# Class-1 tiles of the second mixer product: weights read from w2 itself instead of from a packed copy

## The chip, the core and the metric

The kernel runs on one core of a Trainium2 chip. The metric is the device time of one execution in microseconds. Lower is better. The engines are named as in the profile: PE is TensorE (PEld its weight loads), DVE is VectorE, ACT is ScalarE, POOL is GpSimd and SP is SyncE. SP computes nothing; it issues most of the DMAs. Each engine runs its own list of instructions in an order that is fixed when the program is built. An instruction that waits holds back everything behind it on its engine.

## What is computed

Two layers, each an attention block A and a token mixer B on x of 2048 tokens by 1024 channels (bf16), with the same weights in both layers:

```
x = x + A(layernorm(x), wqkv, wo)     # 32 heads of 32; 8 keys per query, 2 tokens apart
x = x + B(layernorm(x), w1, b1, w2, b2)

def B(x, w1, b1, w2, b2):
    h = layernorm(x)
    u = gelu(einsum("bsd,sf->bdf", h, w1) + b1)     # mixes the 2048 tokens into 3584
    y = einsum("bdf,fs->bds", u, w2) + b2           # and back: w2 is 3584 x 2048
    return y transposed to (token, channel)
```

## The kernel before, in words

**Classes.** A query sees keys two tokens apart, so even tokens (class 0) and odd tokens (class 1) never meet in the attention. The kernel works on the two classes apart, each 1024 tokens in NT = 8 tiles of 128. Column s of w2 belongs to token s, so the class-0 columns of w2 are its even columns and the class-1 columns its odd ones.

**The mixer.** gemm1 (L672) makes g, the 3584 x 1024 activations, in 14 blocks of 256 rows. gemm2_tile(c, i, ...) (L697) makes one output tile: 128 tokens of class c by 1024 channels. It is 28 steps over the 3584 rows with two matmuls each (one per 512 channels), so 56 matmuls. The weights of a step are 128 columns of w2, the moving operand is g. The 28 steps are cut into NW2 = 4 quarters of HF = 7 steps, 14 matmuls each. At the end DVE adds bias and residual out of PSUM (L711), POOL stores the tile (L717), the tile is normalised for the next attention (on ACT with stats_act and norm_act for class-1 tiles 0 to 5, on DVE for the others) and SP issues the transposing DMA to hT (to_hT, L236).

**Where the tiles run.** In layer 0 the eight class-0 tiles of gemm2 run one after the other behind gemm1 (L883). The eight class-1 tiles of layer 0 are held back: they are the fill "second" (second_class, L847) inside the attention of layer 1. There weave (L755), a planner with a modelled time for PE and for DVE, puts the pieces of such fills between the attention's own units, so that PE has work while DVE does the attention's elementwise part. Layer 1's gemm2 (L886) takes both classes of a tile from one load of w2.

**How w2 gets on the chip.** There are two ways:

- w2_tiles(i) (L730) loads 256 neighbouring columns of w2, both classes of tile i, in four DMAs of 448 KB. Each row of such a DMA is 512 bytes. A quarter is one DMA and one buffer. The weights are then read with a step of 2 columns, c::DIL (L741).
- w2_kept(i) (L743) loads the class-1 columns alone from a packed copy in DRAM, w2_odd[i], in two DMAs of 448 KB with rows of 3584 bytes. A DMA covers two quarters. The weights are read without a step.

The packed copy is made on the way: with keep=True, w2_tiles lets ACT copy the odd columns of each quarter into a tile `odd` (L737) and store that to w2_odd[i] from ACT's queue (L740). `odd` takes a buffer of the pool tpl, whose two buffers also serve the attention's T and pr.

**Buffers.** All these loads take buffers from the pool wbp, five of 4 KB per partition, in turn. So do wv (L378), wo (L620) and w1 (L668). A load is issued when the buffer that it is given has been read for the last time. The residual rows xr, the normalised tile hb and others share the pool x2p, four buffers (L79); q, k and v projections of the attention take their weights wq from a pool of their own (wqp, three buffers), and SP issues those loads too (L390).

**Queues.** SP's list holds the loads of w2, w1, wq, wv, wo and xr and the transposing DMAs; POOL's holds the attention's probabilities (pd written at L473, pb read back at L487, 1 MB each) and the stores of output tiles; ACT's holds the stores of `odd`.

Of the kernel before, what the change touches and what calls it, by code (L numbers as in the profile page):

```python
# [15 lines left out]
P = 128  # L16
# [10 lines left out]
def kernel(  # L27
# [21 lines left out]
    NT = SC // P  # L49
# [57 lines left out]
    def bank(name="ps"):  # L107
        return psp.tile([P, 512], FP32, name=name, tag="ps")

    def x2(name, shape=None, dt=BF16):  # L110
        return x2p.tile(shape or [P, D], dt, name=name, tag="x2")
# [61 lines left out]
    xb = [dram.tile([SC, D], BF16, name=f"xb{c}") for c in range(DIL)]  # L173
# [35 lines left out]
    def stats_act(x, mul, eps, junk, sums=None):  # L209

        s1 = sums
        if s1 is None:
            s1 = st("s1", [P, NDC])
            for n in range(NDC):
                nc.scalar.activation(out=junk[:, n * 512:(n + 1) * 512], in_=x[:, n * 512:(n + 1) * 512],  # L215
                                     func=ACT.Identity, accum_out=s1[:, n:n + 1])
        t1 = st("t1", [P, 1])
        nm = st("nm", [P, 1])
        nc.scalar.activation(out=t1[:], in_=s1[:, 1:2], func=ACT.Copy, scale=-1.0 / D)
        nc.scalar.activation(out=nm[:], in_=s1[:, 0:1], func=ACT.Identity, bias=t1[:], scale=-1.0 / D)  # L220
        ss = st("ss", [P, 1])
        nc.scalar.activation(out=junk, in_=x, func=ACT.Square, bias=nm[:], accum_out=ss[:])  # L222
        rs = st("rs", [P, 1])
        rsqrt(rs[:], ss[:], mul / D, eps)
        return nm, rs

    def norm_dve(dst, x, mean, rs, op=ALU.subtract):
        nc.vector.tensor_scalar(out=dst, in0=x, scalar1=mean, scalar2=rs[:], op0=op, op1=ALU.mult)

    def norm_act(dst, x, nm, rs):  # L230
        bi = st("bi", [P, 1])
        nc.scalar.activation(out=bi[:], in_=nm[:], func=ACT.Identity, scale=rs[:])
        nc.scalar.activation(out=dst, in_=x, func=ACT.Identity, bias=bi[:], scale=rs[:])  # L233
# [463 lines left out]
    def gemm2_tile(c, i, w2t, xs, dst, hT, on_act=False, end=False):  # L697
        xo = xs.take()
        halves = [slice(n * 512, (n + 1) * 512) for n in range(NDC)]
        groups = [halves[:1], [slice(512, 768)], [slice(768, 1024)]] if end else [halves]  # L700
        for cols in groups:
            acc = [bank() for _ in cols]
            for n in range(NW2):
                for ft in range(n * HF, (n + 1) * HF):
                    for ps, xc in zip(acc, cols):
                        nc.tensor.matmul(ps[:, 0:xc.stop - xc.start], lhsT=w2t(ft, c),  # L706
                                         rhs=g[ft // GF][:, ft % GF, xc], start=(ft == 0), stop=(ft == FT - 1))
                if n < NW2 - 1:
                    yield 1.5 * len(cols), 0.0
            for ps, xc in zip(acc, cols):  # L710
                nc.vector.scalar_tensor_tensor(out=xo[:, xc], in0=ps[:, 0:xc.stop - xc.start], scalar=b2_sb[:, i, c:c + 1],  # L711
                                               in1=xo[:, xc], op0=ALU.add, op1=ALU.add)
            yield 1.5 * len(cols), 0.75 * len(cols)
            if end:
                nc.sync.dma_start(out=dst[:, cols[0]], in_=xo[:, cols[0]])
        if not end:
            nc.gpsimd.dma_start(out=dst, in_=xo[:])  # L717
        if hT is None:
            return
        hb = x2("hb")  # L720
        if on_act:
            nm, rs = stats_act(xo[:], 1.0, eps1, hb[:])
            norm_act(hb[:], xo[:], nm, rs)
        else:
            mean, rs = stats_dve(xo[:], 1.0, eps1)
            norm_dve(hb[:], xo[:], mean, rs)
        to_hT(hb[:], hT, c, i)
        yield 0.0, 0.0 if on_act else 2.0

    def w2_tiles(i, keep=False):  # L730
        tiles = []
        odd = tpl.tile([P, NW2, HF, P], BF16, name="odd", tag="T") if keep else None
        for n in range(NW2):
            t = wb("w2", [P, HF, FB])
            nc.sync.dma_start(out=t[:], in_=w2_v[:, n * HF:(n + 1) * HF, i * FB:(i + 1) * FB])
            if keep:
                nc.scalar.copy(out=odd[:, n], in_=t[:, :, 1::DIL])  # L737
            tiles.append(t)
        if keep:
            nc.scalar.dma_start(out=w2_odd[i].rearrange("p (f m) -> p f m", m=P), in_=odd[:].rearrange("p n f m -> p (n f) m"))  # L740
        return lambda ft, c: tiles[ft // HF][:, ft % HF, c::DIL]  # L741

    def w2_kept(i):  # L743
        tiles = []
        for n in range(2):
            t = wb("w2", [P, FT // 2, P])
            nc.sync.dma_start(out=t[:].rearrange("p f m -> p (f m)"), in_=w2_odd[i][:, n * F // 2:(n + 1) * F // 2])
            tiles.append(t)
        return lambda ft, c: tiles[ft // (FT // 2)][:, ft % (FT // 2), :]

    def run(*its):
        for _ in chain(*its):
            pass
# [68 lines left out]
    hT = [[None, None] for _ in range(DIL)]  # L822
    new_hT(hT, 0)
    for li in range(2):
        first = li == 0
        at_ = Attn(li, hT, 0 if first else 2)
        h2 = [[None, None] for _ in range(DIL)]
        res = [xin_v[c] for c in range(DIL)] if first else [rows(xb[c]) for c in range(DIL)]

        def clear_pads():  # L830
            for t in v_g:
                nc.gpsimd.memset(t[:, :, 0:PADK + 2], 0.0)

        def opening():
            for i in range(NT):
                x_stage(0, i)
            load_biases()
            clear_pads()
            with tc.manual_schedule(engines={getattr(mybir.EngineType, e) for e in ("PE", "DVE", "Activation", "Pool")}):
                first_tiles(hT, partial(at_.project, 0))  # L840
                for i in range(NT):
                    x_stage(1, i)
            yield "at", 27.0, 29.0
            for u in ((1, 2, 1), (1, 3, 1), (0, 2, 0),):
                yield from at_.proj(0, *u)

        def second_class():  # L847
            new_hT(hT, 1)
            xs = Rows([rows(xa[0][1])[i] for i in range(NT)], 1)
            for i in range(NT):  # L850
                if first:
                    prologue_tile(1, i, hT)
                    yield 0.0, 2.0 * (i % 2 == 0)
                else:
                    yield from gemm2_tile(1, i, w2_kept(i), xs, xb[1][i * P:(i + 1) * P, :], hT, on_act=i < NT - 2)

        def v_ahead():
            if not first:
                clear_pads()
            for pair in range(KD // 2):  # L860
                for unit in at_.proj_pair(1, pair, (2,)):
                    yield 1.75, 0.0

        def partials(lo, hi):
            for fb in range(lo, hi):
                yield from gemm1(h2, fb, (0,), True, False)

        lead = chain(at_.stream(opening() if first else None), out_proj(at_, 1, res[1], xa[li][1], h2, on_act=False))
        weave(lead, {"second": second_class(), "v_ahead": v_ahead(),
                     "out0": out_proj(at_, 0, res[0], xa[li][0], h2, on_act=True),  # L870
                     "partials": partials(0, NFB - KD), "late": partials(NFB - KD, NPART)},
              {"second": 25.0} if first else {})
        for fb in range(NPART, NFB):
            run(gemm1(h2, fb, (0, 1), True, True))
        for fb in range(NPART):
            run(gemm1(h2, fb, (1,), False, True))
        if first:
            with at(top):
                ln_exp_table()
            hT = [[None, None] for _ in range(DIL)]  # L880
            new_hT(hT, 0)
            xs = Rows([rows(xa[0][0])[i] for i in range(NT)], 1)
            for i in range(NT):  # L883
                run(gemm2_tile(0, i, w2_tiles(i, keep=True), xs, xb[0][i * P:(i + 1) * P, :], hT))
        else:
            xs = Rows([rows(xa[1][c])[i] for i in range(NT) for c in range(DIL)], 1)  # L886
            for i in range(NT):
                w2t = w2_tiles(i)
                for c in range(DIL):
                    run(gemm2_tile(c, i, w2t, xs, out_v[c, i], None, end=(i == NT - 1 and c == DIL - 1)))  # L890
# [30 lines left out]
```

## Time and profile before

Four runs gave 1291.75 to 1295.67 us, median 1292.99 us.

| | before |
|---|---|
| profiled execution, its own time | 1292.17 us |
| its span, first to last instruction | 1290.4 us |
| PE busy | 1264.0 us (98%) |
| DVE busy | 680.4 us (53%) |
| ACT busy | 502.7 us (39%) |
| DMA | 173.01 MB, mean 134 GB/s |
| ACT copies to `odd` (L737) | x32, 30.0 us |
| loads by w2_tiles (L735) | x64, 448.0 KB each, median 3.8 us to landing |
| loads by w2_kept (L747) | x16, 448.0 KB each, median 3.8 us to landing |
| stores of `odd` (L740) | x8, 896.0 KB each, median 5.7 us to landing |

How to read it: span is the time from the first to the last instruction, and 1.8 us of the execution lie around it. A row of busy time counts an engine's instructions without the waits between them. The trace gives every time from the start of the span: the class-0 tiles of layer 0 run from 457 us to about 554 us, the class-1 tiles of layer 0 from about 568 us to 748 us.

### The profile page before, as it was taken

The page shows a single profiled execution, that of the slowest core. Times are in us where ns is not written, and L with a number is a line of the kernel's source. Part 1 is how long each engine was busy: PE and PEld are TensorE (multiplying, and loading weights), DVE is VectorE, ACT ScalarE, POOL GpSimd, SP SyncE. Part 2 cuts the span into 40 slices and gives each one's busy share as a digit, 9 for nine tenths or more (in the row PEclk, how much of TensorE's full clock was granted, in tenths as well). Part 3 has the DMA queues.
Part 4 walks back from the last instruction along what each step waited for, and adds up shares of the span by engine and source line. Part 5 has one row for each costly group of instructions (what it writes and reads, how often), then busy time and mean ns, then how long its engine had stood idle before and what let it go on. Part 6 is the DMA issues. An engine that isn't in the chain of part 4 may idle for free. (4 is left out here: it accounts for less than half of the span.)

```text
span 1290.4 us, 15498 instructions
## 1 busy us (share of the span) xinstructions
PE 1264.0 (98%) x6163; PEld 574.9 (45%) x6284; DVE 680.4 (53%) x861; ACT 502.7 (39%) x836; POOL 60.9 (5%) x166
## 2 busy tenths in 40 slices
PE   8999999999999999999999999999999999999999
PEld 4344444444444444444444444444444444444444
DVE  6879899979013422335896734978920233011011
ACT  6845446635324433325414535484343344000000
POOL 3000001001000000000000000010000000000000
PEclk9999999999999999999999999999999999999999
DMA  9852436563422289943647652349262222334331
GB/s 254 187 122 84 120 107 164 165 154 106 139 82 82 60 230 297 288 149 95 156 119 185 158 140 84 73 140 227 67 178 74 74 82 73 122 120 135 104 112 53
DMA packets 217817, 173.01 MB, mean 134 GB/s; under 512 B 32080, under 2 KB 198352, under 8 KB 215696
## 3 DMA queue, kind: packets, MB, share of 16 engines
q1 hardware_dynamic: 206768, 126.11, 36.1%
q0 software_dynamic: 9248, 37.51, 10.5%
q10 hardware_dynamic: 1728, 8.39, 1.7%
q8 instruction: 49, 0.80, 0.3%
q14 instruction: 24, 0.20, 0.0%
HBM read 139.47 MB, written 26.21 MB: 128 GB/s over the span
## 5 line engine op out<-in xcount | busy, mean ns | idle before, releaser
L682 PE MATMUL ps<-h,w 128*128 128x512 bf16 x1756 | 386.7, 379 | 4.8 <-ACT h L233 2.1
L706 PE MATMUL ps<-g,w 128*128 128x512 bf16 (+1 forms) x1785 | 388.0, 376 | 3.0 <-ACT v L419 1.2
L706 PEld LDWEIGHTS <-w 128*128 128x128 bf16 x1820 | 177.5, 98 | 212.4 <-issue 5.6
L682 PEld LDWEIGHTS <-w 128*128 128x128 bf16 x1792 | 175.0, 98 | 215.8 <-issue 4.6
L412 PE MATMUL ps<-hT,wq 128*128 128x512 bf16 (+1 forms) x1085 | 241.4, 374 | 4.3 <-DVE xr L711 0.9
L693 DVE TENSOR_TENSOR tmp<-ps,g 128x512 f32<-128x512 f32 x96 | 66.4, 692 | 211.2 <-PE ps L682 207.0
L711 DVE SCALAR_TENSOR_TENSOR xr<-ps,b_sb,xr 128x512 bf16<-128x512 f32 (+1 forms) x65 | 45.6, 736 | 234.9 <-PE ps L706 196.2
L444 DVE TENSOR_TENSOR T<-q,k 128x4096 bf16<-128x4096 bf16 x60 | 135.5, 2285 | 63.9 <-ACT q L416 52.5
L412 PEld LDWEIGHTS <-wq 128*128 128x128 bf16 x1112 | 108.4, 100 | 132.0 <-issue 13.1
L509 DVE TENSOR_TENSOR pr<-pr 128x2048 bf16<-128x2048 bf16 (+1 forms) x128 | 119.2, 946 | 0.2
L694 ACT ACTIVATE g<-tmp,b_sb 128x512 bf16<-128x512 f32 x96 | 69.2, 721 | 93.2 <-DVE tmp L693 92.8
L412 PE MATMUL ps<-hT,wv 128*128 128x512 bf16 x436 | 100.6, 380 | 1.0 <-issue 0.5
L631 PE MATMUL ps<-wo,oT 128*128 128x512 bf16 x377 | 89.1, 379 | 2.4 <-DMA wo<-in_A_wo_dram 2.0
L688 ACT CAST g<-ps 128x512 bf16<-128x512 f32 x96 | 55.2, 590 | 91.4 <-PE ps L682 85.6
L419 ACT CAST k<-ps 128x1024 bf16<-128x1024 f32 x60 | 60.7, 1014 | 73.5 <-PE ps L412 70.1
L505 DVE TENSOR_TENSOR pr<-pb,v 128x2048 bf16<-128x2048 bf16 x64 | 75.9, 1214 | 20.8 <-DMA pb<-pd 10.8
L505 DVE TENSOR_TENSOR pr<-pb,g 128x2048 bf16<-128x2048 bf16 x64 | 76.3, 1215 | 12.1 <-DMA pb<-pd 12.1
L412 PEld LDWEIGHTS <-wv 128*128 128x128 bf16 x448 | 48.6, 112 | 50.5 <-issue 7.2
L631 PEld LDWEIGHTS <-oT 128*128 128x128 bf16 x384 | 37.2, 98 | 48.4 <-issue 4.3
L416 ACT CAST q<-ps 128x512 bf16<-128x512 f32 x60 | 34.8, 584 | 47.8 <-PE ps L412 47.8
L419 ACT CAST g<-ps 128x1024 bf16<-128x1024 f32 x36 | 36.6, 1016 | 40.9 <-PE ps L412 40.9
L737 ACT COPY odd<-w 128x896 bf16<-128x896 bf16 x32 | 30.0, 937 | 55.1 <-DMA w<-in_B_w_dram 54.9
(91 smaller groups left out, 606.2 us busy)
## 6 DMA issues: line engine op xcount, KB each, us to landing
w<-in_B_w_dram SPq DMA_DIRECT2D x56, 512.0 KB, 4.2
w<-in_B_w_dram SPq DMA_DIRECT2D x64, 448.0 KB, 3.8
wq<-in_A_wqkv_dram SPq DMA_DIRECT2D x38, 512.0 KB, 4.2
pb<-pd POOLq DMA_DIRECT2D x16, 1024.0 KB, 10.3
wo<-in_A_wo_dram SPq DMA_DIRECT2D x16, 512.0 KB, 3.9
xa<-xr POOLq DMA_DIRECT2D x32, 256.0 KB, 3.2
xr<-xa SPq DMA_DIRECT2D x32, 256.0 KB, 3.8
wv<-in_A_wqkv_dram SPq DMA_DIRECT2D x14, 512.0 KB, 5.7
```

The costliest lines, as they stand in the source:

```text
L412: nc.tensor.matmul(ps[:, lo:hi], lhsT=cols, rhs=self.hT[c][hf][:, kt, lo:hi], start=(kt == 0), stop=(kt == KD - 1))
L419: nc.scalar.copy(out=window(buf, 0, PADK + hf * HT, [(KW + 1, 2), (1, HT)]), in_=ps[:].unsqueeze(1).to_broadcast([P, 2, HT]))
L444: nc.vector.tensor_tensor(out=T[:], in0=q.unsqueeze(1).to_broadcast([P, 4, SC]), in1=window(k, par, 2, [(2, 4), (1, SC)]), op=ALU.mult)
L505: nc.vector.tensor_tensor(out=pr[:, :, u, :], in0=pb[:, :, u, :], in1=window(self.v_of(c, dt), par, 2 + hf * HT, [(TB, 4), (2, 4), (1, TB) ...
L509: nc.vector.tensor_tensor(out=pr[:, :, 0:wd, :], in0=pr[:, :, 0:wd, :], in1=pr[:, :, wd:2 * wd, :], op=ALU.add)
L631: nc.tensor.matmul(banks[(i, n)][:], lhsT=at_.oT[c][kt][:, i * P:(i + 1) * P], rhs=wo_t[n][kt // 4][:, kt % 4, :], start=(kt == 0), stop=( ...
L682: nc.tensor.matmul(ps[:], lhsT=wt[c][:, i, fl * P:(fl + 1) * P], rhs=h2[c][i // 4][:, i % 4, dc * 512:(dc + 1) * 512], start=(k == 0), sto ...
L688: nc.scalar.copy(out=gs, in_=ps[:])
L693: nc.vector.tensor_tensor(out=tmp[:], in0=ps[:], in1=gs, op=ALU.add)
L694: nc.scalar.activation(out=gs, in_=tmp[:], func=ACT.Gelu_apprx_tanh, bias=b1_sb[:, ft:ft + 1])
L706: nc.tensor.matmul(ps[:, 0:xc.stop - xc.start], lhsT=w2t(ft, c), rhs=g[ft // GF][:, ft % GF, xc], start=(ft == 0), stop=(ft == FT - 1))
L711: nc.vector.scalar_tensor_tensor(out=xo[:, xc], in0=ps[:, 0:xc.stop - xc.start], scalar=b2_sb[:, i, c:c + 1], in1=xo[:, xc], op0=ALU.add, ...
```

## The change

The class-1 tiles of layer 0 call w2_tiles(i) in place of w2_kept(i), and the class-0 tiles call it without keep. So nothing is packed and nothing is stored to w2_odd, and the class-1 tiles load 256 columns of w2 in four DMAs and read every second column. The functions themselves are as before; w2_kept and the packing branch are called by nothing any more.

```diff
@@ second_class @@
-                    yield from gemm2_tile(1, i, w2_kept(i), xs, xb[1][i * P:(i + 1) * P, :], hT, on_act=i < NT - 2)
+                    yield from gemm2_tile(1, i, w2_tiles(i), xs, xb[1][i * P:(i + 1) * P, :], hT, on_act=i < NT - 2)
@@ layer 0, behind gemm1 @@
-                run(gemm2_tile(0, i, w2_tiles(i, keep=True), xs, xb[0][i * P:(i + 1) * P, :], hT))
+                run(gemm2_tile(0, i, w2_tiles(i), xs, xb[0][i * P:(i + 1) * P, :], hT))
```

## The prediction

> **What bounds the kernel now.** First the page, for the engine that is never idle.
>
> ```profile
> PE 1264.0 (98%) x6163; PEld 574.9 (45%) x6284; DVE 680.4 (53%) x861; ACT 502.7 (39%) x836; POOL 60.9 (5%) x166
> ```
>
> PE is the bound, and busy means at its pace: the timeline has 49 matmuls in 10.74 us, 0.219 us each, wherever it runs freely. So an edit counts only by what PE waits. Next, busy time by stage: class-0 tiles; layer 1's attention with the class-1 tiles, cut in four.
>
> ```profile
> 460.00:550.00 90.00, 89.58 (x410) 40.80 (x417) 23.49 (x42) 29.19 (x43) 3.78 (x7) 1.00 1.00 281
> 555.00:640.00 85.00, 83.29 (x440) 35.82 (x447) 51.10 (x45) 36.86 (x53) 2.77 (x5) 1.00 0.47 125
> 640.00:675.00 35.00, 34.20 (x177) 15.21 (x180) 34.06 (x38) 5.63 (x6) 1.02 (x2) 1.00 0.33 103
> 675.00:700.00 25.00, 24.45 (x112) 11.63 (x114) 14.98 (x19) 13.63 (x28) 1.76 (x4) 1.00 0.98 229
> 700.00:757.00 57.00, 55.27 (x251) 25.39 (x255) 34.63 (x46) 22.86 (x48) 3.63 (x13) 1.00 0.60 161
> ```
>
> Columns: stretch, length, then busy us of PE, PEld, DVE, ACT, POOL; clock; DMA share; GB/s. In the first row the DMA engines are full (1.00) while PE loses 0.42 us in 90. In the other four it loses 1.71 + 0.80 + 0.55 + 1.73 = 4.79 us. Third, PE's waits in 555 to 760 us (us in all, times, longest):
>
> ```profile
> PE ps L706 <- ACT v L419: 1.2, 2, 0.7
> PE ps L412 <- DVE xr L711: 0.9, 1, 0.9
> PE ps L412 <- DMA wq<-in_A_wqkv_dram: 0.9, 1, 0.9
> ```
>
> None is for a w2 load. Fourth, SP's timeline, which the change fills (start, length, line, what, count):
>
> ```profile
> 680.16 0.32 SPq L747 DMA_DIRECT2D w<-w2o  x1
> 682.32 3.35 SPq L236 DMA_TRANSPOSE hT<-hb  x1
> 690.92 0.33 SPq L608 DMA_DIRECT2D xr<-xa  x1
> ...
> 698.96 0.32 SPq L608 DMA_DIRECT2D xr<-xa  x1
> 713.60 1.24 SPq L236 DMA_TRANSPOSE hT<-hb  x1
> 714.94 0.52 SPq L747 DMA_DIRECT2D w<-w2o  x1
> ...
> 725.63 0.34 SPq L608 DMA_DIRECT2D xr<-xa  x1
> 736.42 1.23 SPq L236 DMA_TRANSPOSE hT<-hb  x1
> ```
>
> SP stands still from 699.3 to 713.6 us and from 726.0 to 736.4 us. The cause, from SP's waits in 560 to 757 us:
>
> ```profile
> SPq L236 <- ACT hb L233: 32.4, 5, 14.3
> ```
>
> The transposing DMA of a tile waits for its normalised hb; that waits for L711 on DVE, which is behind with the attention (34.06 of 35 us busy). A w2 load listed behind such a transpose waits too.
>
> **The change, part by part.**
>
> *Removed: packing.* 32 copies of 0.937 us take 30.0 us off ACT, 8 stores of 896 KB leave its queue, and `odd` leaves the pool of T. All this lies beside the class-0 tiles, where PE loses 0.42 us: that is the most it gives. I take 0. There the DMA should fall from 281 GB/s by 7.3 MB in 90 us, 82 GB/s, to some 200.
>
> *Weights at a step of two columns.* PE's count is unchanged, 448 matmuls. The trace has both forms, first class 0 (step 2) in 460 to 550 us, then class 1 (packed) in 655 to 673 us:
>
> ```profile
> L706 PEld LDWEIGHTS <-w 128*128 128x128 bf16 x417 | 40.8, 98 | 49.2
> L706 PEld LDWEIGHTS <-w 128*128 128x128 bf16 x84 | 8.2, 98 | 9.9
> ```
>
> Behind the bar stand busy us and mean ns: 98 ns both, under a pace of 219 ns. Cost 0. Only wv's step of 4 shows a dearer load (page: 112 ns), still below the pace.
>
> *Added: bytes.* 32 loads of 448 KB for 16: 7.3 MB more, all in 555 to 757 us, where 28 MB move now (560 to 757 us). At the full-DMA row's 281 GB/s that is 26 us of DMA in 202 us at about half use. Only 675 to 700 us has no room (0.98). About 1.4 MB more should fall there (12 loads for the 6 from 659 to 697 us; half of the surplus lands in it), 5 us at 281 GB/s. There ACT already waits 5.0 us for a store of xb behind the two pb loads, and holds the v casts that PE waits 1.2 us for. Bounds on PE: 0 (buffers absorb it) to 5 us. I take 0: of the 10.1 us that this store needs now, PE shows about 1 us.
>
> The Trainium skill, "DMA: Bandwidth & Descriptors", Specifications, speaks against any cost of short rows: a transfer of 512 B or more runs at line rate, about 27 GiB/s per engine. By that estimate the extra bytes need 16 us of 16 engines instead of the 26 us above; this case's full-DMA row, 281 GB/s with rows of mostly 512 B, does not reach that rate, so the row decides.
>
> *Added: SP's issues.* 32 at 0.37 us for 16 at 0.34 us is 6.4 us more on a queue that waits most of the time. Cost 0 by itself.
>
> *Moved: the lead of a load.* This is the term I keep. All loads take wbp's five buffers in turn. A load waits until the one five before it is used up, so its lead is four loads' worth of PE work: four halves, 56 x 2 x 0.216 = 24.2 us, before; four quarters, 12.1 us, after. The load lands 3.8 us after issue (at most 6.6 us by w2_tiles, 9.8 us by w2_kept). So SP may be 8.3 us late before PE waits. Before, it could be 20.4 us late.
>
> In the class-0 stage the same five buffers serve the same loads at full pace and PE waits for none, but there hb is normalised by an idle DVE and SP's longest wait on hb is 2.6 us. Here the holds are 14.3 and 10.4 us. I follow the ring by hand from the counts of L706 in PE's timeline, quarters of 14 matmuls, tiles numbered from 0.
>
> - Hold to 713.6 us. Tile 4's first quarter is used up at 694.0 us; its buffer is for tile 5's second quarter, needed at 714.8 us. Ahead of the held transpose it lands by 702 us. Behind it: 713.6 + 1.3 + 3.7 = 718.6 us, 3.8 us late. The next quarters (buffers free at 697.0 and 699.9 us) would land about 719 and 720 us, needed at 717.8 and 720.8 us: hidden by the first delay.
> - Hold to 736.4 us. Tile 6's first quarter is used up at 726.8 us, just after the hold begins; its buffer is for tile 7's second quarter, needed at 738.9 us. Behind the hold: 736.4 + 1.3 + 5 (between the 3.7 us of L747 and the 6.1 us of the wv beside it) = 742.7 us, 3.8 us late.
> - Hold from 685.7 to 694.9 us (xr, then a transpose). The load of tile 4's last quarter can go at 696.2 us, lands at 700.5 us, is needed at 703.5 us: in time.
>
> Each is late only if the new list puts the load behind the transpose. That list is not in the trace. For: before, the loads at 714.94 and 723.54 us stand right behind a transpose although the first one's buffer was free at 706.3 us. Against: a quarter's load comes due more often, so some find a place ahead. Bounds: 0, and both, 7.6 us. I take one, **3.8 us**, as the row before shows both orders.
>
> Sum on the profiled execution: 1292.2 + 0 + 0 + 0 + 3.8 = **1296.0 us**, 3.0 us above the median of 1293.0 us (the execution lies 0.8 us below that).
>
> **The rivals.** A measurement here tells about 0.2%, 2.6 us, from no change.
>
> 1. *No load is late.* The loads stand ahead of the held transposes, as five buffers suffice in the class-0 stage; PE's waits stay as they are. 1292.2 + 0 = 1292 to 1293 us. For it: no PE wait for w2 anywhere in 455 to 760 us. Against: holds above the 8.3 us allowance.
> 2. *Faster: the stage's waits for banks go.* PE's waits around 675 and 711 us come from class-1 tiles whose xr and hb hold up DVE and ACT while PE runs ahead. A later arrival of w2 spaces these tiles; with packing gone the lists are also made anew. Price: at most the 4.8 us that PE loses in the stage, 1292.2 - 4.8 = 1287.4 us; with the two waits on L419 and the one on L711 gone as the gaps in the rows show, 1.2 + 0.9 plus the refill of its pace, about 3 us, 1289 us. It decides if the first tiles, at 640 to 675 us, are spread and not bunched. Against: the order of the fills in weave uses the same modelled costs.
> 3. *The DMA burst at 675 to 700 us decides as well.* Both loads late and the burst's 5 us: 1292.2 + 7.6 + 5 = 1304.8 us. For: 0.98 use there. Against: 0.47 and 0.33 before it, so loads can go early.
>
> **How the numbers follow.** Forecast (one or two loads late) 0.42; rival 1 0.32; rival 2 0.18; rival 3 0.08. Faster by over 0.2% is rival 2: 0.18. Within it is rival 1: 0.32. Slower is the forecast and rival 3: 0.50. The range goes from 1289 us, rival 2's likelier price, to 1305 us, rival 3. The forecast's own range is 1294.8 to 1300 us (2.6 to 7.6 us).
>
> **What would show it.** No L737 and no L740; w2 loads x96 by L735; weight loads of L706 at 98 ns in both stages; DMA in the class-0 stage near 200 GB/s and PE idle there under 0.5 us. In 640 to 757 us a wait of PE for DMA w<-in_B_w_dram of 3 to 8 us in one or two pieces, each behind a late transpose in SP's timeline. I am wrong if PE's waits in 555 to 760 us hold no w2 load, if the time moves outside that stretch, or if L706's loads go above the pace.

## The result, and the profile after

| | before | after |
|---|---|---|
| median of the runs (lowest to highest) | 1294.6 us (1291.75 to 1300.39, 69 runs) | 1297.1 us (1294.83 to 1301.41, 45 runs) |
| ratio, 95% interval | | 1.0020 [1.0014, 1.0025] |
| profiled execution, its own time | 1292.17 us | 1297.12 us |
| its span | 1290.4 us | 1295.0 us |

The change costs 0.20%, 2.5 us. The two profiled executions differ by more, 4.6 us of span: the one of before lies near the low end of its runs. So the profiles say where time goes, and the runs how much: sums by place below are against that one execution of before and come out larger than the change in the runs.

The page of after, in the rows that answer to those of before:

```profile
PE 1264.7 (98%) x6163; PEld 574.8 (44%) x6284; DVE 680.5 (53%) x861; ACT 473.9 (37%) x804; POOL 60.9 (5%) x166
...
L706 PEld LDWEIGHTS <-w 128*128 128x128 bf16 x1820 | 177.3, 98 | 215.2 <-issue 7.2
...
w<-in_B_w_dram SPq DMA_DIRECT2D x96, 448.0 KB, 3.8
```

ACT's busy time fell by 28.8 us (the packing), PE's work is the same, a weight load of the mixer takes 98 ns, and all 96 loads of w2 come from w2 itself. The busy time by stage of after, in the same stretches and columns as before:

```profile
460.00:550.00 90.00, 89.58 (x411) 40.78 (x418) 23.49 (x42) 3.49 (x14) 3.78 (x7) 1.00 0.80 215
555.00:640.00 85.00, 82.94 (x439) 35.61 (x446) 51.12 (x45) 37.01 (x53) 2.77 (x5) 1.00 0.52 136
640.00:675.00 35.00, 34.05 (x176) 15.18 (x179) 33.67 (x37) 5.47 (x6) 0.63 (x1) 1.00 0.50 147
675.00:700.00 25.00, 23.66 (x108) 11.23 (x110) 11.99 (x16) 13.64 (x28) 2.15 (x4) 1.00 1.04 238
700.00:757.00 57.00, 52.96 (x240) 24.02 (x244) 37.47 (x49) 21.69 (x46) 3.64 (x13) 1.00 0.87 225
```

In the class-0 stage the DMA fell from 281 to 215 GB/s and PE gained nothing. In the class-1 stage PE loses 2.06 + 0.95 + 1.34 + 4.04 = 8.39 us where it lost 4.79 us, 3.1 of the 3.6 us of increase behind 675 us. PE's waits of after in 640 to 770 us (us in all, times, longest):

```profile
PE ps L706 <- ACT v L419: 2.5, 3, 0.9
PE ps L412 <- DVE xr L711: 2.2, 2, 1.3
PE ps L706 <- DMA w<-in_B_w_dram: 0.7, 1, 0.7
```

A load of w2 is now late, but by 0.7 us only. The waits for ACT and DVE grew instead, from 1.2 and 0.9 us. Where, says PE's timeline, first of before, then of after:

```profile
685.15 15.27 PE L706 MATMUL ps<-g,w 128*128 128x512 bf16 x69
...
706.73 3.62 PE L412 MATMUL ps<-hT,wq 128*128 128x512 bf16 x16
710.83 0.38 PE L706 MATMUL ps<-g,w 128*128 128x512 bf16 x1 [0.48 <-ACT v L419]
711.92 36.20 PE L706 MATMUL ps<-g,w 128*128 128x512 bf16 x164 [0.72 <-ACT v L419]
```

```profile
684.99 6.42 PE L706 MATMUL ps<-g,w 128*128 128x512 bf16 x29
692.36 9.01 PE L706 MATMUL ps<-g,w 128*128 128x512 bf16 x40 [0.95 <-ACT v L419]
...
709.17 3.61 PE L412 MATMUL ps<-hT,wq 128*128 128x512 bf16 x16 [1.32 <-DVE xr L711]
713.66 0.38 PE L706 MATMUL ps<-g,w 128*128 128x512 bf16 x1 [0.87 <-ACT v L419]
714.75 30.46 PE L706 MATMUL ps<-g,w 128*128 128x512 bf16 x136 [0.72 <-ACT v L419]
745.95 6.22 PE L706 MATMUL ps<-g,w 128*128 128x512 bf16 x28 [0.73 <-DMA w<-in_B_w_dram]
```

PE's list has the same order in both kernels, so its 6284 weight loads can be paired and their starts subtracted. After minus before is -0.5 us until 630 us and -0.15 us from there to 690 us. Then it jumps: +1.11 at 692.4, +1.49 at 709.2, +0.39 at 713.7, +0.3 at 730, +0.9 at 746, +0.39 at 759.7 us, together 4.6 us; behind that only 0.2 us more comes. So, against this execution of before, PE loses in two places: **2.99 us at 692 to 714 us** (the burst), and **1.6 us at 730 to 760 us** (late quarters and what follows them). I call these sums the first and the second step.

**The second step** is in SP's timeline of after:

```profile
731.85 0.39 SPq L735 DMA_DIRECT2D w<-in_B_w_dram  x1
739.25 1.23 SPq L236 DMA_TRANSPOSE hT<-hb  x1
740.58 1.19 SPq L735 DMA_DIRECT2D w<-in_B_w_dram  x2
```

The load at 731.85 us is tile 7's second quarter: it found a place ahead of the held transpose. The third quarter stands behind it, goes at 740.6 us and lands at 745.9 us, 0.7 us after PE was ready. The 0.3 us at 730 us is tile 6's second quarter, which took 8.2 us to land among two loads of wq. Tile 5's four quarters all stand ahead of the transpose held to 716.42 us and are in time.

**The first step** begins at the two pb loads of 1 MB and what is in flight beside them. SP's timeline of before, then of after:

```profile
665.27 6.36 SPq L747 DMA_DIRECT2D w<-w2o  x2
671.68 0.46 SPq L608 DMA_DIRECT2D xr<-xa  x1
```

```profile
662.10 12.45 SPq L735 DMA_DIRECT2D w<-in_B_w_dram  x5
674.60 0.55 SPq L608 DMA_DIRECT2D xr<-xa  x1
680.01 0.37 SPq L735 DMA_DIRECT2D w<-in_B_w_dram  x1
```

Before, SP issues a half at 671.3 us and xr right behind it; the next half must wait until 680.2 us. They land at 675.9 and 676.5 us, 1.3 and 1.9 us behind the start of the first pb load (674.6 us; the second starts at 675.1 us). After, five quarters fill the ring; the last of them goes when a quarter is used up at 674.2 us, and xr, listed behind it, at 674.6 us. They land at 678.2 and 679.4 us, 2.5 and 3.6 us behind the start of the first pb load (675.7 us; the second starts at 676.2 us). pb starts 1.1 us later here because pd, which it reads, landed at 675.2 and not at 674.1 us; in the second profile of after (below) it starts at 674.6 us, and the step is there all the same. The DMA queues of before, then of after, in 676 to 679 us (q0 is POOL's, q1 SP's; packets, MB, share of the DMA engines' time):

```profile
q0 software_dynamic: 84, 0.69, 96.1%
q1 hardware_dynamic: 5, 0.00, 0.4%
```

```profile
q1 hardware_dynamic: 880, 0.63, 65.8%
q0 software_dynamic: 38, 0.31, 43.8%
```

In these 3 us POOL's queue, with pb, moves less than half of what it moved before. The two pb loads land at 684.4 and 688.5 us (before 681.7 and 686.3), the first store of xb behind them at 689.6 us (before 687.0). ACT's timeline of before, then of after:

```profile
687.25 0.63 ACT L215 ACTIVATE hb<-xr 128x512 bf16<-128x512 bf16 x1 [4.95 <-DMA xb<-xr]
...
688.49 0.99 ACT L419 CAST v<-ps 128x1024 bf16<-128x1024 f32 x1
```

```profile
690.08 0.63 ACT L215 ACTIVATE hb<-xr 128x512 bf16<-128x512 bf16 x1 [7.93 <-DMA xb<-xr]
...
691.32 0.99 ACT L419 CAST v<-ps 128x1024 bf16<-128x1024 f32 x1
```

hb takes a buffer of x2p that the stored xr still holds, so ACT stands until the store has landed and goes on 2.8 us later than before. The v casts behind it have nothing to do with that store, but ACT's list is in order. They free PE's banks (the wait at 692.36 us) and feed DVE (after):

```profile
684.48 1.23 DVE L505 TENSOR_TENSOR pr<-pb,v 128x2048 bf16<-128x2048 bf16 x1 [6.34 <-DMA pb<-pd]
692.35 2.36 DVE L505 TENSOR_TENSOR pr<-pb,v 128x2048 bf16<-128x2048 bf16 x2 [6.63 <-ACT v L419]
```

Both lines start 2.7 to 2.8 us later than before (681.81 and 689.51 us). DVE has no slack there, so L711 of a class-1 tile comes later and PE waits 1.32 us for it at 709.17 us.

### The profile page after: what moved, and what is told of

It reads as the page before. It is cut to its first block, busy times and chain, and to the rows that moved or that the text cites. A ratio compares the mean times of both kernels' runs of the same rounds, so it can differ in the third digit from the quotient of the medians.

```text
span 1295.0 us, 15457 instructions
## 1 busy us (share of the span) xinstructions
PE 1264.7 (98%) x6163; PEld 574.8 (44%) x6284; DVE 680.5 (53%) x861; ACT 473.9 (37%) x804; POOL 60.9 (5%) x166
## 5 line engine op out<-in xcount | busy, mean ns | idle before, releaser
L711 DVE SCALAR_TENSOR_TENSOR xr<-ps,b_sb,xr 128x512 bf16<-128x512 f32 (+1 forms) x65 | 45.6, 737 | 251.6 <-PE ps L706 219.6
L195 ACT ACTIVATE ln<-mv,eps 128x1 f32<-128x1 f32 x29 | 8.5, 293 | 93.2 <-DVE mv L204 85.7
```

## The experiments

The ratio is always to the kernel before on the same chip. Edits are shown against the kernel after, with `...` where code is left out; where two kernels are named, the same edit is made in both. Five of the runs read other elements of w2 in some or all class-1 tiles, as their expectations say. "First step" and "second step" are the jumps of PE's weight loads against the profile of before, summed over 690 to 715 us and over 715 to 760 us. "Last w2" is the last load of w2 issued ahead of 679 us. The run with copies added is 7.6 us late when it reaches the stage; its times are given less 7.6 us.

| run | last w2, xr issued at | pb lands | first xb lands | first step | second step | ratio |
|---|---|---|---|---|---|---|
| before | 671.3, 671.7 | 681.7, 686.3 | 687.0 | 0 | 0 | 1 |
| after | 674.2, 674.6 | 684.4, 688.5 | 689.6 | 2.99 | 1.60 | 1.0020 [1.0014, 1.0025] |
| after, once more | 674.1, 674.5 | 683.8, 689.4 | 690.0 | 3.49 | 1.29 | 1.0028 [1.0016, 1.0041] |
| packing kept, unused | 673.5, 673.9 | 683.2, 688.8 | 689.4 | 3.22 | 1.09 | 1.0015 [1.0004, 1.0027] |
| quarters of half the bytes | 674.1, 674.5 | 682.3, 687.3 | 689.6 | 3.04 | 0 | 1.0018 [1.0009, 1.0027] |
| halves, no packing | 671.6, 671.9 | 682.2, 686.9 | 687.6 | 0.63 | 0.21 | 0.9998 [0.9988, 1.0007] |
| halves, copies added | 671.3, 671.7 | 681.9, 686.6 | 689.1 | 2.37 | 0.29 | 1.0065 [1.0049, 1.0082] |
| halves, then quarters | 672.6, 673.0 | 683.1, 687.7 | 688.2 | 0.20 | 1.59 | 1.0015 [1.0006, 1.0024] |
| quarters, then halves | 673.6, 674.0 | 682.4, 689.1 | 690.4 | 4.80 | 0 | 1.0026 [1.0017, 1.0035] |

**Packing put back, its copy read by nobody.**

```diff
-                run(gemm2_tile(0, i, w2_tiles(i), xs, ...))
+                run(gemm2_tile(0, i, w2_tiles(i, keep=True), xs, ...))
```

> The changed kernel with the packing put back: ACT copies the odd columns and stores them, and nothing reads them. Class-1 tiles load as in the changed kernel. Theory (bytes: the 7.3 MB more between 640 and 720 us delay the pb loads and the xb stores, so DVE and ACT are late and PE waits for them): as the changed kernel, some 2.5 us above before, since the packing lies in another stage. Rival (lead: a quarter's load arrives late behind a held transpose): the same, 2.5 us. Third (the packing's going is what moves the time): 0 us against before. PE's gaps at 685 to 770 us should be those of the changed kernel, 4 to 5 us in all by the profile.

Its class-0 stage has the DMA at 1.00 and 280 GB/s again, and PE is busy for 90.00 of 90 us there. The steps stand where they stood in after. So removing the packing moves nothing that these runs can tell.

**Quarters with half the bytes.** Four loads of 224 KB, rows of 1792 bytes, from w2 itself.

```diff
+    def w2_quarters(i):
+        ...
+        for n in range(NW2):
+            t = wb("w2", [P, HF, P])
+            nc.sync.dma_start(out=..., in_=B_w2[(i + 8 * n // 4) * P:(i + 8 * n // 4 + 1) * P, 0:HF * P])
+            ...
...
-                    yield from gemm2_tile(1, i, w2_tiles(i), xs, ...)
+                    yield from gemm2_tile(1, i, w2_quarters(i), xs, ...)
```

> No packing; a class-1 tile takes four loads of 224 KB in rows of 1792 bytes, so it has the changed kernel's ring of quarters (lead 12.1 us) and before's bytes. It reads other elements of w2 than the class-1 columns, so these tiles are not the reference's. Theory (bytes): as before, within 0.7 us, and the row 675 to 757 us loses no more than before (2.3 us). Rival (lead): as the changed kernel, 2.5 us above before, with late quarters behind transposes.

The first step is all there: 1.16 at 692.4, 1.49 at 709.2, 0.39 at 713.7 us. My theory up to here, that the surplus of bytes fills the burst, fell with this run. But no quarter is late: tile 7's third goes at 740.6 us as in after and lands in 3.8 us instead of 5.3. So no late load makes the first step either; what the two kernels share is SP's list and with it the times 674.1 and 674.5 us. The store of xb is late with them (689.6 us), although the second pb lands only 1.1 us later than in before.

**Halves without packing.**

```diff
-            nc.sync.dma_start(out=..., in_=w2_odd[i][:, n * F // 2:(n + 1) * F // 2])
+            nc.sync.dma_start(out=..., in_=B_w2[(2 * i + n) * P:(2 * i + n + 1) * P, 0:F // 2])
...
-                    yield from gemm2_tile(1, i, w2_tiles(i), xs, ...)
+                    yield from gemm2_tile(1, i, w2_kept(i), xs, ...)
```

> No packing; a class-1 tile takes two loads of 448 KB in rows of 3584 bytes, as before, but from w2 itself, so before's lead and before's bytes without the packing. It reads other elements of w2 than the class-1 columns. Theory (bytes) and rival (lead) both: as before, 0 us, or up to 0.5 us under it. Third (the packing's going moves the time): 2.5 us above before.

The time is that of before, with the packing gone, and the steps are small: 0.63 and 0.21 us. So the cost lies in loading by quarters.

**Halves, with the bytes added elsewhere.** As the run before; beside it two copies of 448 KB per tile from w2 to w2_odd in rows of 512 bytes, which nobody reads.

```diff
+                        if k in (0, 2):
+                            nc.sync.dma_start(out=spare[:, k // 2 * HF:(k // 2 + 1) * HF, :],
+                                              in_=w2_v[:, k * HF:(k + 1) * HF, i * FB:(i + 1) * FB])
```

> As e3_halves, and each class-1 tile also issues two copies of 448 KB in rows of 512 bytes from w2 to a DRAM tensor that nobody reads: before's lead with the changed kernel's bytes. It reads other elements of w2 than the class-1 columns. Theory (bytes): 2 to 4 us above before, with PE's gaps at ACT v L419 and DVE xr L711 as in the changed kernel. Rival (lead): as before, within 0.7 us.

Ratio 1.0065 [1.0049, 1.0082], and it does not answer the question it was made for: the copies wait for no buffer, so all 16 were issued at 20.5 to 54.1 us, in layer 0, far from the stage. There 7.6 us are lost.

But its profile shows something on the first step. In the stage the issues stand as in before, 7.6 us later: w2 and xr go 3.3 and 2.9 us ahead of pb, and pb lands within 0.3 us of before's times. Yet the first store of xb took 12.2 us instead of 10.1 us, and 2.37 us of the first step are there. ACT's timeline of this run, then PE's:

```profile
697.21 0.63 ACT L215 ACTIVATE hb<-xr 128x512 bf16<-128x512 bf16 x1 [7.31 <-DMA xb<-xr]
```

```profile
699.50 9.01 PE L706 MATMUL ps<-g,w 128*128 128x512 bf16 x41 [0.33 <-ACT v L419]
...
716.31 3.61 PE L412 MATMUL ps<-hT,wq 128*128 128x512 bf16 x16 [1.33 <-DVE xr L711]
```

So a late store is enough for the step, without quarters, without moved issues and without a late pb. Why the store was late here is not shown.

**The store of class-1 tiles 0 to 5 from ACT's queue**, in after and in before. The theory was that the store is late because it stands behind pb on POOL's queue.

```diff
-            nc.gpsimd.dma_start(out=dst, in_=xo[:])
+            (nc.scalar if on_act else nc.gpsimd).dma_start(out=dst, in_=xo[:])
```

> The changed kernel with one edit: class-1 tiles 0 to 5 are stored to xb from ACT's queue and not from POOL's, so the store no longer stands behind the two pb loads. Theory (chain: w2 and xr loads in flight when the pb loads start push the burst out; the xb store behind them lands 2.7 us later; hb gets its buffer later; ACT's v casts, listed behind hb, are later; DVE's pv and with it L711 is later; PE waits for banks at 692, 709 and 714 us): the steps at 692 and 709 us vanish, 2.5 to 4 us under the changed kernel, so 0 to 1.5 us under before; a late w2 quarter near 746 us stays (0.9 us). Rival (PE's steps come from late w2 quarters or from pb itself, not through xb): as the changed kernel, 2.5 us above before.

> The kernel before with the same edit, class-1 tiles 0 to 5 stored from ACT's queue. Theory (chain): ACT's 5.0 us wait for the xb store goes, PE's waits at 711 and 712 us (1.5 us) too: 0.5 to 1.5 us under before, and at most 1 us better than e6_after_store_act. Rival: as before, within 0.5 us, 2.5 us better than e6_after_store_act.

Ratios 1.0047 [1.0031, 1.0064] and 1.0045 [1.0027, 1.0063]. In both, the first step is gone, and so are the waits that before itself has there (the shift against before falls by 1.5 us). But in both PE loses 8.7 us elsewhere, between 600 and 640 us, most of it in one wait (7.4 us in the second). SP's timeline of the second, and PE's:

```profile
612.90 1.23 SPq L236 DMA_TRANSPOSE hT<-hb  x1
614.24 8.82 SPq L390 DMA_DIRECT2D wq<-in_A_wqkv_dram  x3
```

```profile
629.09 0.61 PE L412 MATMUL ps<-hT,wq 128*128 128x512 bf16 x1 [7.41 <-DMA wq<-in_A_wqkv_dram]
```

Tile 0's transpose goes 1.4 us later than in before, and the wq load behind it at 614.24 instead of 613.49 us. The pb loads of that time start at 614.4 us. In before wq was 1.3 us ahead of them and landed after 4.7 us; here it is 0.2 us ahead and lands after 14.8 us, with the second pb. So a load can be held up by the burst too, where in the first step it is pb and the store that are late.

**Only tiles 1 and 2 stored from ACT's queue**, in after and in before.

```diff
-            nc.gpsimd.dma_start(out=dst, in_=xo[:])
+            (nc.scalar if on_act and i in (1, 2) else nc.gpsimd).dma_start(out=dst, in_=xo[:])
```

> The changed kernel with the stores of class-1 tiles 1 and 2 alone on ACT's queue; tile 0 stays on POOL's, so that its transpose, and the wq load behind it at 613 us, are issued as before. Theory (chain through the xb store and ACT's list): PE's steps at 692, 709 and 714 us (3.0 us together) and the two waits of before at 711 and 712 us (1.5 us) go, a late quarter near 746 us may stay: 3 to 4.5 us under the changed kernel, 0 to 1.5 us under before. Rival (the steps come from elsewhere): 2.5 us above before.

> The kernel before with the stores of class-1 tiles 1 and 2 alone on ACT's queue. Theory (chain): PE's waits at 711 and 712 us go, no wait of 7.5 us for wq near 630 us as in e7_before_store_act: 1 to 1.5 us under before, within 1 us of e8_after_store12_act. Rival: as before, within 0.5 us.

Ratios 0.9988 [0.9977, 0.9999] and 0.9984 [0.9975, 0.9992]: the second is the fastest version found, 0.16% below before. But the reason is not that the store lands sooner. ACT's timeline of the first:

```profile
682.03 1.02 ACT L419 CAST v<-ps 128x1024 bf16<-128x1024 f32 x1 [0.62 <-PE ps L412]
...
684.09 1.00 ACT L419 CAST v<-ps 128x1024 bf16<-128x1024 f32 x1
689.75 0.63 ACT L215 ACTIVATE hb<-xr 128x512 bf16<-128x512 bf16 x1 [4.66 <-DMA xb<-xr]
```

The store lands at 689.6 us, as late as in after, 12.8 us after its issue. What changed is ACT's list: two v casts now stand ahead of the hb that waits for the store. The lists of DVE and PE are those of after. So the queue of the store is not the cause, and the wait of hb on ACT costs PE only through the casts behind it. The Trainium skill, "DMA: Bandwidth & Descriptors", "Issuing engines are not separate DMA queues", says that all issuing engines share the same 16 DMA engines; 12.8 us from either queue agrees.

**Quarters for some tiles only.** The first run loads halves for tiles 0 to 3 and quarters for 4 to 7, the second the other way round. They decide between two theories: what is in flight when pb starts, or quarters as such in the tiles that PE works on from 690 us.

```diff
-            nc.sync.dma_start(out=..., in_=w2_odd[i][:, n * F // 2:(n + 1) * F // 2])
+            nc.sync.dma_start(out=..., in_=B_w2[(2 * i + n) * P:(2 * i + n + 1) * P, 0:F // 2])
...
-                    yield from gemm2_tile(1, i, w2_tiles(i), xs, ...)
+                    yield from gemm2_tile(1, i, w2_tiles(i) if i >= 4 else w2_kept(i), xs, ...)
```

> The changed kernel, but only class-1 tiles 4 to 7 load quarters of 256 columns; tiles 0 to 3 load two halves of 448 KB with long rows out of w2 itself (other elements of w2 than the reference, so those four tiles compute something else). Theory (what is in flight when the two pb loads start): with halves so far, the third quarter of tile 4 goes at 671.3 us with xr behind it and the next at 680.2 us, as in the kernel before; so pb lands near 681.7 and 686.3 us, the first xb store near 687 us, and the 1.1 us at 692 and the 1.5 us at 709 us are not lost, although all loads from tile 4 on are quarters of 512-byte rows. What may stay is the late quarter of tile 7, 0.7 to 3.8 us at 739 to 746 us. Time 1.0 to 2.5 us below the changed kernel, ratio to the kernel before 1.000 to 1.0015. Rival (the quarters as such, in the tiles that PE works on from 690 us, cost it: shorter lead, shorter rows): both steps stay, ratio 1.002.

> The mirror of the run before: class-1 tiles 0 to 3 load quarters of 256 columns as in the changed kernel, tiles 4 to 7 load two halves of 448 KB with long rows out of w2 itself (other elements of w2, so these four tiles compute something else). Theory (what is in flight when the two pb loads start): the fifth load before tile 4's second half is a quarter of tile 3, used up at 674.2 us, so that load goes at 674.2 us and xr behind it at 674.6 us, as in the changed kernel; the steps of 1.1 us at 692 and 1.5 us at 709 us stay although the tiles at that time read long rows, and the late quarter at 746 us goes. Ratio to the kernel before 1.001 to 1.002. Rival (the quarters in the tiles from 690 us on cost it): both steps go, ratio 1.000.

PE's timeline of halves, then quarters:

```profile
686.39 15.27 PE L706 MATMUL ps<-g,w 128*128 128x512 bf16 x70
...
707.97 3.62 PE L412 MATMUL ps<-hT,wq 128*128 128x512 bf16 x16
...
744.51 6.22 PE L706 MATMUL ps<-g,w 128*128 128x512 bf16 x28 [0.98 <-DMA w<-in_B_w_dram]
```

and of quarters, then halves:

```profile
693.23 9.01 PE L706 MATMUL ps<-g,w 128*128 128x512 bf16 x41 [2.76 <-ACT v L419]
...
710.04 3.61 PE L412 MATMUL ps<-hT,wq 128*128 128x512 bf16 x16 [1.33 <-DVE xr L711]
...
715.62 36.20 PE L706 MATMUL ps<-g,w 128*128 128x512 bf16 x167 [0.72 <-ACT v L419]
```

The two steps come apart. Halves up to tile 3 give back the old moment: the third quarter of tile 4 goes at 672.6 us, the fourth not before 681.4 us, and the first step is 0.20 us, with quarters of 512-byte rows from tile 4 on. Quarters up to tile 3 give the first step, 4.80 us, though all loads from tile 4 on are halves with long rows. Here w2 and xr are issued within 0.5 us of the first pb (673.6 and 674.0 against 673.5 us). That alone does not make it larger than in after: in three other runs they are within 0.6 us of pb as well, and the step is 3.0 to 3.5 us. The second step behaves the other way: it needs quarters in tiles 6 and 7. The first run's ratio, 1.0015, is at the upper end of what was expected: its second step alone is 1.6 us, and its profile has 0.9 us from layer 0, which no edit touches.

Taken together: all five profiles with quarters up to tile 3 have the first step, 2.99 to 4.80 us. Of the four with halves there, three have 0 to 0.63 us, and the run with copies added has 2.37 us. In all nine of the table the step goes with the store of xb: measured against PE's own shift, it lands at most 0.4 us later than in before where the step is 0 to 0.63 us, and 2.1 to 4.5 us later where the step is 2.37 to 4.80 us. So the path from the late store to PE is shown. That quarters make the store late, by the moment at which w2 and xr go out, is what nine profiles fit but for one; it is not the only thing that does.

**The changed kernel once more**, for the places of its steps.

> The changed kernel unaltered, on the same chip as e8_after_store12_act and e9_before_store12_act and once more profiled. All theories: 2 to 3 us above before. If the steps at 692, 709 and 714 us come from the lists and not from chance, this profile has them again at the same places.

1.61 at 692.8, 1.49 at 709.6, 0.39 at 714.1, 0.4 at 730.5, 0.6 at 746.1, 0.31 at 759.8 us: the same places.

## Why the prediction was right or wrong

- **The number.** 1296.0 us was 3.8 us above the profiled execution; the profile of after stands 4.95 us above it, and the runs say 2.5 us. Sign and size hold, but the size by luck: by the profiles the term that was kept gave 1.6 us instead of 3.8 us, and a term put at 0 gave 2.99 us.
- **Packing, 0**: right, and the DMA fell to 215 GB/s where some 200 was said. The run with the packing put back shows it.
- **Weights at a step of two, 0**: right, 98 ns.
- **Added bytes, 0 of 0 to 5 us**: this is the step that failed. The place (675 to 700 us) and the path (store of xb, hb on ACT, v casts, PE) were named, and 2.99 us lies in the bounds. It was put at 0 because PE showed only 1 us of a 10.1 us store; but the store was already the one that ACT and DVE waited for last, so its extra 2.7 us passed on whole. The cause within it was wrong too: half the bytes give the same step. The 1.4 MB of surplus that I put into this stretch did not come: its rows show 238 GB/s against 229, some 0.2 MB in 25 us. I did not ask which load is issued in the last 2 us ahead of pb; the two mixed runs speak for that moment, the run with copies added shows that the store can be late without it.
- **SP's issues, 0**: right as a sum of issue times; but it is SP's list, with xr behind the last free quarter, that moves the issues with which the first step comes.
- **The lead of a load, 3.8 us**: the mechanism was right, the term mis-sized: 1.6 us with all that follows. Of the two holds, the one to 713.6 us made no load late. At the other, the second quarter stood ahead and the third behind; it is needed a quarter, 3.1 us, later than the second. By before's times it would come 0.7 us late instead of 3.8; measured 0.7 us of waiting in after and 0.98 us where the first step is away. The run with loads of half the bytes, in rows of 1792 bytes, lands 1.5 us sooner and has none.
- **Rival 1** (no load late) fell by the wait of 0.7 us, and still 3 us would have been lost. **Rival 2** fell: its three waits grew, from 1.2 + 0.9 to 2.5 + 2.2 us. **Rival 3** had both mechanisms and sizes too large for both. The stretch and the kind of signs were right: a w2 wait behind a held transpose, below the 3 to 8 us named.

Left open: what makes the store of xb late. The moment at which w2 and xr are issued goes with it in eight of nine profiles, was not tried for each of the two loads, and does not explain the run with copies added. Open too is how often an execution of before has such a late store: there is one profile of it, 2.4 us below the median of its runs, and that may be why the steps add up to 4.6 us where the runs differ by 2.5 us. A further buffer in x2p or wbp was not tried.

## What to carry to other kernels

Ask of a changed load not only whether it lands in time, but what is still in flight when the next large transfer starts, and which instruction on an in-order engine waits for what lands last in that burst: by the profiles this cost more here (2.99 us) than the late load (1.6 us). Cutting loads finer without more buffers shortens the lead and moves every later issue on that queue; here halving the bytes of these loads left the first step as it was. One profile of a kernel is one execution: a difference of 2 us in one landing can be there without the change. Where an engine waits for a buffer, see that what others need stands ahead of it in its list; here a list with two v casts ahead of such a wait went with 0.16% on the kernel before and some 0.4% on the kernel after (1292.05 against 1297.14 us on one chip).

## What the runs showed of the hardware

- A load of 512 KB issued 1.3 us ahead of two 1 MB loads landed after 4.7 us; issued 0.2 us ahead of them, after 14.8 us. It is no rule that the nearer load loses: at the next burst a quarter of 448 KB issued 0.5 us ahead of pb (after, once more) and a half issued 0.1 us behind it (quarters, then halves) landed after 3.8 and 4.3 us. A store of 256 KB took 10 to 15 us in such a burst, from POOL's or ACT's queue alike (the median over the whole kernel is 3.9 us in before).
- Queues are served side by side, not in the order of issue: in 676 to 679 us of after, SP's queue held 65.8% and POOL's 43.8% of the engines' time. The Trainium skill, "DMA: Bandwidth & Descriptors", "Queues, rings and completion order", says that a DMA engine goes round its queues packet by packet. The trace agrees on the sharing; 880 records of one queue against 38 of the other do not look like turns of one record each, and no run here shows how many records a turn has.
- Bytes and rows of a load: a 448 KB quarter with rows of 512 bytes took 5.3 us to land at 740 us, the 224 KB quarter with rows of 1792 bytes 3.8 us at the same place, where bytes and rows differ at once. With equal bytes, 448 KB at 652 to 669 us, it was 3.5 to 3.7 us with rows of 512 bytes (after) and 3.2 to 3.6 us with rows of 3584 bytes (before).
